# A complex linear attention feeding a mixture of experts on one core: ScalarE's list set by hand through the first attention, first scores in two halves, eight weights by transfers, other steps for the attention of groups four and five

## The chip, the core and the metric

The kernel runs on one core of a Trainium2 chip. Five engines work from queues of their own: TensorE (PE, matrix products; its weight loads are shown apart as PEld), VectorE (DVE), ScalarE (ACT), GpSimd (POOL) and SyncE (SP, which here only issues DMA transfers). The metric is the device time of one execution in microseconds, with the inputs in the chip's memory; three runs of the kernel before took 1015.36 to 1018.92 us, median 1017.08.

## The reference

For each of 4 batches and 8 heads a complex state of 48 x 48 is rotated by a normalised factor at each of 768 steps and takes in one product of a key and a value; the output is the real part read by the query. The outputs of all heads, side by side, are 3072 tokens of 384 features, which go through four dense experts, weighted by normalised probabilities.

```python
scale = np.minimum(mag, 0.999) / (mag + 1e-06)        # mag = sqrt(a_re**2 + a_im**2)
for t in range(S):
    new_re = ar * S_re - ai * S_im
    new_im = ar * S_im + ai * S_re
    S_re, S_im = (new_re + kv, new_im)                # kv = k_t outer v_t
    y[:, :, t] = np.einsum('bhd,bhde->bhe', q[:, :, t], S_re)
...
for e in range(E):
    h = np.maximum(x @ w1[e], 0.0)
    out += p[:, e:e + 1] * (h @ w2[e])
```

## The kernel before

**Products in three parts.** Each fp32 operand of an expert is kept as a rounded high part and a rest (whi and wlo, xha and xla, hh and hl), and each product is three products on TensorE: high with high, rest with high, high with rest. The 16 weight blocks of the first two experts are loaded at the start. Nine of them (NPRE) come by a plain load into wst; split_w casts them on ScalarE (whi, L138), forms the rest on TensorE (lp, the block times the identity minus whi, L147 and L150) and copies it back on ScalarE (wlo, L151). The other seven come by transfers that cast on the way (cast_w), and their rest is formed by a negated copy on ScalarE (L131) on which a second transfer adds the block (add_w).

**Attention in chunks.** The 3072 tokens are 12 groups of 256 tokens, each of two chunks of 128. The front of a group is element-wise. `norm` squares the factors and forms the normalising scale (Ln, Exp and others on ScalarE, the rest on VectorE). `prefix` multiplies the factors along the sequence on VectorE, where pf are its first steps. The head of `finish` forms Q (L425) and the tail K (L441). For groups 2 and later, Q and K go through DRAM (q_d, k_d) by SyncE's transfers and come back with heads on partitions (Qst, Kst); for groups 0 and 1 TensorE turns them instead (qp, and kp with the copy to Kst, L497). Each chunk then has these products on TensorE: ktp (the key turned, L487, copied to KT by ScalarE), dp (the state's increment, L505, subtracted into G), sc (scores, L517, masked by VectorE into scs) and yp (values, L531 and L536, copied to y by ScalarE, L543). For groups 0 to 2, xp (L567) turns y into xha; later groups take y through DRAM into xa. t_factors copies the factors with which `rotate` turns G for the next chunk or group.

**MoE.** moe1 runs experts 0 and 1 over blocks of 256 tokens, one per group, in eight steps: 18 products ph (L179), the rectified copy hh on ScalarE, its rest hl on VectorE, and 12 products po (L198) of a step before. After the 12 blocks of moe1, moe2 runs experts 2 and 3 in blocks of 512 tokens (phb L817, pob L830).

**What sets the order.** The front and the attention of group g run during block g - 1. `between(k)` is called ahead of step k of the block: it advances the front by an estimated cost of STEP per step, and in the steps from FIRST[g] on (2 where the table has no entry) it emits one piece of attention g, of three. Within that, a scheduler with a cost model decides the order in which each engine issues its instructions, except where `behind(a, b)` demands that a is issued after b, on whatever engines they are. Each engine then works through its list strictly in that order, so an instruction that waits holds all behind it. The table WARM names, for some of the last plainly loaded weights, a product of group 0's attention behind which the lp products are put.

The attention of group 0 has nothing beside it, as its output is the first input of the MoE. Between its two chunks stand, on ScalarE, the copies of wlo 6 to 8, the norm of group 1 (tiles s1, u1) and the copies of the attention itself.

Of the kernel before, what the change touches and what calls it, by code (L numbers as in the profile page):

```python
# [15 lines left out]
B, H, S, D = 4, 8, 768, 48  # L16
# [39 lines left out]
NPRE = 9  # L56
WARM = {6: "pq", 7: "tk", 8: "tk1"}
NSEL = 2
XSEL = 3
FIRST = {1: 5, 2: 5, 3: 4, 4: 3}  # L60
# [8 lines left out]
def fast_path(ctx, tc, qkP, aP, vP, probsP, w, out, flag):  # L69
# [159 lines left out]
    with ExitStack() as c1:  # L229
# [81 lines left out]

        def norm(g, A, parts=((0, SEG),), prev=(None, None)):
            s = tmp(f"s{g}")
            u = tmp(f"u{g}")
            for n, (lo, hi) in enumerate(parts):
# [15 lines left out]
                nc.scalar.activation(L, m2, AF.Ln, bias=m2b)  # L331
                exp = nc.scalar.activation(y0, L, AF.Exp, scale=-0.5, bias=lnb)
                if g == 0:
                    nc.vector.tensor_tensor(v, m2, y0, op=ALU.mult)
                    nc.vector.scalar_tensor_tensor(v, v, 4.0 / CAP ** 2, y0, op0=ALU.mult, op1=ALU.mult)
                else:
                    nc.scalar.activation(v, y0, AF.Square, scale=2.0 / CAP)
                    nc.vector.tensor_tensor(v, m2, v, op=ALU.mult)
                nc.scalar.activation(L, y0, AF.Identity, scale=2.0 * EPS / CAP, bias=neg1)
# [50 lines left out]
        def finish(g, A, qk):  # L390
# [24 lines left out]
            def head(lo, hi):  # L415
# [8 lines left out]
                for c in range(2):  # L424
                    ins = nc.vector.tensor_tensor(dst(Q[:, c, :, :C], lo, hi), rows(A[:, c], lo, hi),  # L425
                                                  rows(qk[:, 0], lo, hi), op=ALU.mult)
                    if g < NSEL and lo == 1:
                        behind(ins, red)
                if hi == CG:
                    nc.scalar.activation(Q[:, :, :, C].rearrange("p c (j n) -> p c j n", n=CG),  # L430
                                         A[:, :, SEG - 1, NS - 1::NS].unsqueeze(3).broadcast_to([P, 2, NJ, CG]),
                                         AF.Copy)
# [28 lines left out]
        def t_factors(g):  # L461
            Tr, Ti = Qst[0:D, :, CG - 1, C:], Qst[IM:M, :, CG - 1, C:]
            ins = nc.scalar.activation(TA[0:D], Tr, AF.Copy)
            tc.keep_in_program_order(ins)
            behind(ins, state["y", g])
            tc.keep_in_program_order(nc.scalar.activation(TA[IM:M], Tr, AF.Copy))
            tc.keep_in_program_order(nc.scalar.activation(TB[IM:M], Ti, AF.Copy))
            tc.keep_in_program_order(nc.scalar.activation(TB[0:D], Ti, AF.Copy, scale=-1.0))
# [3 lines left out]
        def chunk(g, c, K, y):  # L472
# [8 lines left out]
            def turned():  # L481
                if last and g >= NSEL:
                    return
                for i in range(2):
                    kt_ps = ps_a.tile([P, HD], F32, tag="pa", name=f"ktp{g}_{c}_{i}")
                    for j in range(NJ):
                        ins = nc.tensor.transpose(kt_ps[:, j * P:(j + 1) * P], K[:, i, j * CG + c, :], ident)  # L487
                    nc.scalar.activation(KT[:, :, i * IM:i * IM + D],
                                         kt_ps.rearrange("p (h d) -> p h d", d=D), AF.Copy)
# [23 lines left out]
            def scores():  # L513
                for hf in range(2):
                    s_ps = ps_a.tile([P, 4, C], F32, tag="pa", name=f"sc{g}_{c}_{hf}")
                    for h in range(4):
                        nc.tensor.matmul(s_ps[:, h, :], Kc[:, hf * 4 + h, :], Qc[:, hf * 4 + h, :],  # L517
                                         start=True, stop=True)
# [4 lines left out]
            def values():  # L523
# [18 lines left out]
                for us in ((slice(0, M),) if g < XSEL else (slice(0, D), slice(IM, M))):  # L542
                    state["y", g] = nc.scalar.activation(y[us, :, cs], y_ps[us], AF.Copy)  # L543
# [27 lines left out]
        def near_attention(g, QK):  # L571
# [12 lines left out]
            sc0()  # L584
# [3 lines left out]
            state["tk1"] = turn1()  # L588
# [69 lines left out]
        for _ in norm(0, A[0], parts=halves):  # L658
            pass
        cuts = (1, NS // CG, NS)  # L660

        todo, last = {}, {}
# [64 lines left out]
        for i in range(NPRE):  # L727
            split_w(i, wst[i] if i in wst else stage1(i, PRE), ((ps_o, "po"), (ps_h, "ph")),
                    prev_pe=state.get(WARM.get(i)), prev_lo=state["kst", 0, 0] if i in WARM else None)
# [7 lines left out]
        behind(nc.vector.reduce_sum(prs, pr, axis=mybir.AxisListType.X), last["dve"])  # L737
# [320 lines left out]
```

## Time and profile before

| | before |
|---|---|
| median of three runs | 1017.08 us (1015.36 to 1018.92) |
| the profiled execution | 1015.63 us |
| its span | 1013.9 us |
| TensorE busy | 982.5 us (97%), 6624 products |
| VectorE busy | 591.2 us (58%) |
| ScalarE busy | 363.4 us (36%) |
| first product of the MoE (ph) starts | 57.20 us |
| last wait of TensorE on another engine or a transfer | 0.93 us, ahead of 268.28 us |

A row of the timeline has the start and the duration in us, the engine, the line, the operation, the tiles out<-in, their shapes, and in brackets the idle time of the engine ahead of it with what ended it. A row of the chain of waits has start, duration and what was done; "issue" is time in which the engine waited for nothing that the profile shows. The windows view gives, for each stretch, its length, the busy time and number of instructions of five engines, the granted clock of TensorE (1.00 is full speed), the share of the DMA engines and what they moved in GB/s. Rows of consecutive equal instructions are drawn together (x16), and a duration then runs from the first start to the last end.

### The profile page before, as it was taken

How to read it: one execution, taken by the hardware profiler on the slowest of the kernel's cores; microseconds unless marked ns; L12 is line 12 of the kernel's file. 1: busy time of each engine (PE TensorE's matmuls, PEld its weight loads, DVE VectorE, ACT ScalarE, POOL GpSimd, SP SyncE). 2: the span in 40 equal slices, each digit the busy share in tenths (PEclk: the TensorE clock that was granted, in tenths of full speed). 3: DMA queues.
4: the chain of work that ended last, by engine and by line, in shares of the span. 5: the costliest groups of instructions: out<-in, count | busy, mean ns of one | idle time of the engine just before them, and what ended most of it. 6: DMA issues, size and time to landing. Idle time of an engine off the chain costs nothing.

```text
span 1013.9 us, 16212 instructions
## 1 busy us (share of the span) xinstructions
PE 982.5 (97%) x6624; PEld 924.4 (91%) x6624; DVE 591.2 (58%) x1219; ACT 363.4 (36%) x653; POOL 34.4 (3%) x64
## 2 busy tenths in 40 slices
PE   4799999999999999999999999999999999999997
PEld 2699999999999999999999999989999999999996
DVE  6798988989797989888842363232232222321221
ACT  7746526436263553636332343121111211211110
POOL 5020000000000000000000000000000000000000
PEclk9899999999999999999999999999999999999999
DMA  9474356474554837457171691021030010100001
GB/s 318 148 147 150 82 154 155 154 184 125 149 164 119 213 99 196 129 145 198 54 164 33 232 334 41 1 88 38 1 125 1 32 63 1 63 1 1 32 1 35
DMA packets 78932, 110.78 MB, mean 109 GB/s; under 512 B 5440, under 2 KB 63344, under 8 KB 78848
## 3 DMA queue, kind: packets, MB, share of 16 engines
q1 hardware_dynamic: 74560, 94.53, 32.6%
q0 software_dynamic: 4288, 15.13, 5.0%
q8 instruction: 54, 0.88, 0.4%
q14 instruction: 30, 0.25, 0.1%
HBM read 73.71 MB, written 35.92 MB: 108 GB/s over the span
## 4 chain that ended last, share of the span: by engine, by line
PE 87%; DVE 4%; DMA 3%; ACT 2%; issue 1%; SPq 0%; DVEq 0%; ACTq 0%
PE pob L830 20%; PE phb L817 20%; PE ph L179 18%; PE po L198 17%; PE sc L517 5%; PE dp L505 2%; PE yp L536 2%; PE yp L531 2%; DMA Kst<-k_d 2%; PE ktp L487 1%; PE xp L567 1%; DMA k_d<-K 1%; DVE K L441 1%; PE qp L385 0%; DVE hl L189 0%
## 5 line engine op out<-in xcount | busy, mean ns | idle before, releaser
L823 DVE SCALAR_TENSOR_TENSOR hlb<-phb,hhb 128x512 fp32r<-128x512 f32 x96 | 66.4, 691 | 270.6 <-ACT hhb L822 270.6
L822 ACT ACTIVATE hhb<-phb 128x512 fp32r<-128x512 f32 x96 | 57.4, 598 | 314.6 <-PE phb L817 299.2
L830 PE MATMUL pob<-wlo,hhb 128*128 128x384 f32 x384 | 129.2, 337 | 0.0
L198 PE MATMUL po<-whi,hh 128*128 128x384 f32 x384 | 129.0, 338 | 0.0
L830 PE MATMUL pob<-whi,hhb 128*128 128x384 f32 x384 | 128.9, 336 | 0.0
L198 PE MATMUL po<-wlo,hh 128*128 128x384 f32 x384 | 128.8, 335 | 0.0
L198 PE MATMUL po<-whi,hl 128*128 128x384 f32 x384 | 124.4, 338 | 0.2 <-DVE hl L189 0.2
L830 PE MATMUL pob<-whi,hlb 128*128 128x384 f32 x384 | 120.4, 336 | 0.0
L188 ACT ACTIVATE hh<-ph 128x512 fp32r<-128x512 f32 x96 | 57.2, 596 | 158.3 <-PE ph L179 158.0
L179 PE MATMUL ph<-xha,whi 128*128 128x256 f32 x576 | 104.9, 287 | 0.8 <-ACT xha L166 0.8
L179 PE MATMUL ph<-xha,wlo 128*128 128x256 f32 x576 | 101.3, 283 | 0.0
L179 PE MATMUL ph<-xla,whi 128*128 128x256 f32 x576 | 101.0, 283 | 0.0
L189 DVE SCALAR_TENSOR_TENSOR hl<-ph,hh 128x512 fp32r<-128x512 f32 x96 | 66.1, 688 | 53.5 <-ACT hh L188 53.0
L817 PE MATMUL phb<-xhb,whi 128*128 128x512 f32 x288 | 91.8, 392 | 0.0
L179 PEld LDWEIGHTS ph<-xha,whi 128*128 128x128 f32 x576 | 86.1, 190 | 1.8 <-ACT xha L166 1.0
L179 PEld LDWEIGHTS ph<-xha,wlo 128*128 128x128 f32 x576 | 82.8, 190 | 0.5 <-issue 0.5
L179 PEld LDWEIGHTS ph<-xla,whi 128*128 128x128 f32 x576 | 82.8, 191 | 0.0
L817 PE MATMUL phb<-xlb,whi 128*128 128x512 f32 x288 | 82.7, 392 | 0.0
L817 PE MATMUL phb<-xhb,wlo 128*128 128x512 f32 x288 | 82.3, 393 | 0.0
L830 PEld LDWEIGHTS pob<-whi,hhb 128*128 128x128 f32 x384 | 72.1, 188 | 3.7
L830 PEld LDWEIGHTS pob<-wlo,hhb 128*128 128x128 f32 x384 | 72.1, 188 | 3.3
L198 PEld LDWEIGHTS po<-whi,hh 128*128 128x128 f32 x384 | 72.5, 189 | 0.5 <-issue 0.3
(165 smaller groups left out, 1574.8 us busy)
## 6 DMA issues: line engine op xcount, KB each, us to landing
wst<-w SPq DMA_DIRECT2D x25, 384.0 KB, 6.4
qk<-qkP SPq DMA_DIRECT2D x24, 384.0 KB, 6.5
acc_d<-acc POOLq DMA_DIRECT2D x24, 384.0 KB, 4.4
prev<-acc_d SPq DMA_DIRECT2D x24, 384.0 KB, 4.9
A<-aP SPq DMA_DIRECT2D x22, 384.0 KB, 7.9
q_d<-Q SPq DMA_DIRECT2D x20, 387.0 KB, 3.6
Qst<-q_d SPq DMA_DIRECT2D x20, 387.0 KB, 5.2
k_d<-K SPq DMA_DIRECT2D x16, 384.0 KB, 3.4
```

Source lines behind the costliest of these rows:

```text
L179: ins = nc.tensor.matmul(ph[:, u, :], wt[:, j * P:(j + 1) * P], xt[:, j, :], start=(n == 0), stop=(n == 3 * NJ - 1))
L188: wts["hh"] = nc.scalar.activation(hh, ph, AF.Relu)
L189: nc.vector.scalar_tensor_tensor(hl, ph, 0.0, hh, op0=ALU.max, op1=ALU.subtract)
L198: nc.tensor.matmul(po[t], ht[:, u, t * P:(t + 1) * P], wt[:, HD:], start=(i % FE == 0 and n == 0), stop=(i % FE == FE - 1 and n == 2))
L505: nc.tensor.matmul(d_ps[:, h, :], KT[:, h, :], vc[:, h * D:(h + 1) * D], start=True, stop=True)
L517: nc.tensor.matmul(s_ps[:, h, :], Kc[:, hf * 4 + h, :], Qc[:, hf * 4 + h, :], start=True, stop=True)
L531: ins = nc.tensor.matmul(yo, st[:, o:o + n], Qc[:, o // D, :], start=True, stop=False)
L536: ins = nc.tensor.matmul(yo, vc[:, o:o + n], sc[h // 4][:, h % 4, :], start=first, stop=True)
L817: nc.tensor.matmul(ph, wt[:, j * P:(j + 1) * P], xt[:, j, :], start=(n == 0), stop=(n == 3 * NJ - 1))
L822: nc.scalar.activation(hh, ph, AF.Relu)
L823: nc.vector.scalar_tensor_tensor(hl, ph, 0.0, hh, op0=ALU.max, op1=ALU.subtract)
L830: ins = nc.tensor.matmul(po[t], ht[:, t * P:(t + 1) * P], wt[:, HD:], start=(i % FE == 0 and n == 0), stop=(i % FE == FE - 1 and n == 2))
```

## The change

Four things are changed. On ScalarE, Ln and Exp of group 1's norm are put behind the copy KT of group 0's second chunk and behind y of its first chunk; the first weights' casts are put behind the norm of group 0; and the copies of wlo 6 and 7 are put behind y of the first chunk. In the norm of group 0 the second half of the factors takes ScalarE's square in place of one of two operations of VectorE. The factors of t_factors are behind the copy y of a named chunk, and the sum of probabilities is put behind Q of group 1's head (`last["qp"]`). In group 0 the scores of the first chunk are issued in two halves of four heads, the second behind the turn of the second key. Eight weight blocks in place of nine are split on the chip, and eight in place of seven come by transfers. FIRST puts the attention of group 4 at step 4 in place of 3, and that of group 5 at step 3 in place of 2.

```diff
@@ -53,11 +53,11 @@
 PRE = ("acc", "xh", "xl")
 MID = ("x", "xh", "xl")
 AHEAD = 6
-NPRE = 9
-WARM = {6: "pq", 7: "tk", 8: "tk1"}
+NPRE = 8
+WARM = {6: "pq", 7: "tk"}
 NSEL = 2
 XSEL = 3
-FIRST = {1: 5, 2: 5, 3: 4, 4: 3}
+FIRST = {1: 5, 2: 5, 3: 4, 4: 4, 5: 3}
 STEP = 3.4
 MORE = (1.9, 1.9, 0.5)
 HALF = (2, 3)
@@ -309,6 +309,8 @@
             nc.vector.tensor_tensor(x[:, 0], v1[:, 0], v2[:, 1], op=ALU.subtract)
             nc.vector.tensor_tensor(x[:, 1], v1[:, 1], v2[:, 0], op=ALU.add)
 
+        last = {}
+
         def norm(g, A, parts=((0, SEG),), prev=(None, None)):
             s = tmp(f"s{g}")
             u = tmp(f"u{g}")
@@ -328,15 +330,18 @@
                     behind(ins[0], exp)
                     behind(sq, exp)
                 yield 1.0
-                nc.scalar.activation(L, m2, AF.Ln, bias=m2b)
+                ln = nc.scalar.activation(L, m2, AF.Ln, bias=m2b)
                 exp = nc.scalar.activation(y0, L, AF.Exp, scale=-0.5, bias=lnb)
-                if g == 0:
+                if g == 1:
+                    behind(ln, state["kt", 0, 1])
+                    behind(exp, state["y", 0, 0])
+                if g == 0 and n == 0:
                     nc.vector.tensor_tensor(v, m2, y0, op=ALU.mult)
                     nc.vector.scalar_tensor_tensor(v, v, 4.0 / CAP ** 2, y0, op0=ALU.mult, op1=ALU.mult)
                 else:
                     nc.scalar.activation(v, y0, AF.Square, scale=2.0 / CAP)
                     nc.vector.tensor_tensor(v, m2, v, op=ALU.mult)
-                nc.scalar.activation(L, y0, AF.Identity, scale=2.0 * EPS / CAP, bias=neg1)
+                last["lin"] = nc.scalar.activation(L, y0, AF.Identity, scale=2.0 * EPS / CAP, bias=neg1)
                 yield 0.95
                 nc.vector.scalar_tensor_tensor(y0, v, 3.0, y0, op0=ALU.subtract, op1=ALU.mult)
                 yield 0.95
@@ -426,6 +431,7 @@
                                                   rows(qk[:, 0], lo, hi), op=ALU.mult)
                     if g < NSEL and lo == 1:
                         behind(ins, red)
+                        last["qp"] = ins
                 if hi == CG:
                     nc.scalar.activation(Q[:, :, :, C].rearrange("p c (j n) -> p c j n", n=CG),
                                          A[:, :, SEG - 1, NS - 1::NS].unsqueeze(3).broadcast_to([P, 2, NJ, CG]),
@@ -462,7 +468,7 @@
             Tr, Ti = Qst[0:D, :, CG - 1, C:], Qst[IM:M, :, CG - 1, C:]
             ins = nc.scalar.activation(TA[0:D], Tr, AF.Copy)
             tc.keep_in_program_order(ins)
-            behind(ins, state["y", g])
+            behind(ins, state["y", g, CG - 1 if g < NSEL else 0])
             tc.keep_in_program_order(nc.scalar.activation(TA[IM:M], Tr, AF.Copy))
             tc.keep_in_program_order(nc.scalar.activation(TB[IM:M], Ti, AF.Copy))
             tc.keep_in_program_order(nc.scalar.activation(TB[0:D], Ti, AF.Copy, scale=-1.0))
@@ -485,8 +491,8 @@
                     kt_ps = ps_a.tile([P, HD], F32, tag="pa", name=f"ktp{g}_{c}_{i}")
                     for j in range(NJ):
                         ins = nc.tensor.transpose(kt_ps[:, j * P:(j + 1) * P], K[:, i, j * CG + c, :], ident)
-                    nc.scalar.activation(KT[:, :, i * IM:i * IM + D],
-                                         kt_ps.rearrange("p (h d) -> p h d", d=D), AF.Copy)
+                    state["kt", g, c] = nc.scalar.activation(KT[:, :, i * IM:i * IM + D],
+                                                             kt_ps.rearrange("p (h d) -> p h d", d=D), AF.Copy)
                 return ins
 
             def turned_back():
@@ -510,12 +516,14 @@
                     nc.vector.tensor_tensor(Gt, state[g, c], d_ps, op=ALU.subtract)
                 state[g, c + 1] = Gt
 
-            def scores():
-                for hf in range(2):
+            def scores(halves=(0, 1), prev=None):
+                for hf in halves:
                     s_ps = ps_a.tile([P, 4, C], F32, tag="pa", name=f"sc{g}_{c}_{hf}")
                     for h in range(4):
-                        nc.tensor.matmul(s_ps[:, h, :], Kc[:, hf * 4 + h, :], Qc[:, hf * 4 + h, :],
-                                         start=True, stop=True)
+                        ins = nc.tensor.matmul(s_ps[:, h, :], Kc[:, hf * 4 + h, :], Qc[:, hf * 4 + h, :],
+                                               start=True, stop=True)
+                        if h == 0 and prev is not None:
+                            behind(ins, prev)
                     s_sb = small.tile([P, 4, C], F32, tag="sc", name=f"scs{g}_{c}_{hf}", bufs=4)
                     nc.vector.tensor_tensor(s_sb, s_ps, maskp.unsqueeze(1).broadcast_to([P, 4, C]), op=ALU.mult)
                     sc.append(s_sb)
@@ -540,7 +548,7 @@
                 if g == 0:
                     state["pe"] = ins
                 for us in ((slice(0, M),) if g < XSEL else (slice(0, D), slice(IM, M))):
-                    state["y", g] = nc.scalar.activation(y[us, :, cs], y_ps[us], AF.Copy)
+                    state["y", g, c] = nc.scalar.activation(y[us, :, cs], y_ps[us], AF.Copy)
 
             return turned, turned_back, increment, scores, values
 
@@ -581,11 +589,15 @@
             state["tk"] = turn0()
             state["bk"] = back0()
             inc0()
-            sc0()
+            sc0((0,))
+            if g > 0:
+                sc0((1,))
             yield
             if g == 0:
                 yield trip(f"q_d{g}", Q, Qst, 1)()
-            state["tk1"] = turn1()
+            tk = turn1()
+            if g == 0:
+                sc0((1,), tk)
             back1()
             val0()
             sc1()
@@ -657,9 +669,10 @@
         A.append(load_a(1))
         for _ in norm(0, A[0], parts=halves):
             pass
+        lin = last["lin"]
         cuts = (1, NS // CG, NS)
 
-        todo, last = {}, {}
+        todo = {}
 
         def front(g, A, qk):
             pre = prefix(g, A, cuts if g < NSEL else (1, NS))
@@ -725,8 +738,8 @@
         for _ in norm(1, A[1], prev=(state["kst", 0, 0], last["dve"])):
             pass
         for i in range(NPRE):
-            split_w(i, wst[i] if i in wst else stage1(i, PRE), ((ps_o, "po"), (ps_h, "ph")),
-                    prev_pe=state.get(WARM.get(i)), prev_lo=state["kst", 0, 0] if i in WARM else None)
+            split_w(i, wst[i] if i in wst else stage1(i, PRE), ((ps_o, "po"), (ps_h, "ph")), prev=lin,
+                    prev_pe=state.get(WARM.get(i)), prev_lo=state["y", 0, 0] if i in WARM else None)
         tick = big.tile([1, 1], F32, name="tick")
         nc.gpsimd.tensor_copy(tick, Qst[0:1, 0, 1, 0:1])
         for i in range(NPRE, NF1):
@@ -734,7 +747,7 @@
         x[0] = split_x(0, x[0])
         for _ in todo.pop(0):
             pass
-        behind(nc.vector.reduce_sum(prs, pr, axis=mybir.AxisListType.X), last["dve"])
+        behind(nc.vector.reduce_sum(prs, pr, axis=mybir.AxisListType.X), last["qp"])
         nc.vector.tensor_scalar(prs, prs, 1e-9, None, op0=ALU.add)
         nc.vector.reciprocal(prs, prs)
         nc.vector.tensor_tensor(pr, pr, prs.unsqueeze(2).broadcast_to([P, NT // P, E]), op=ALU.mult)
```

Lines of the kernel after stand 2 to 8 further down than those of before (L331 is L333, L339 is L344, L343 is L348, L488 is L494, L497 is L503, L517 is L523, L543 is L551).

The first place is ScalarE near the start of the program, before, from the linear term of the first half of group 0's norm on (s0 and u0 are the norm's tiles, whi the weights' high parts, lnb and neg1 constants):

```order
L339 ACTIVATE s0_207<-u0_208,neg1_83 128x384
L138 ACTIVATE whi0_502<-wst0_185 128x768
L331 ACTIVATE s0_207<-s0_207,m2b_89 128x384
L138 ACTIVATE whi1_513<-wst1_187 128x768
L343 ACTIVATE u0_208,st_w_161<-u0_208,neg1_83 128x384
L332 ACTIVATE u0_208<-s0_207,lnb_85 128x384
L138 ACTIVATE whi2_524<-wst2_189 128x768
L138 ACTIVATE whi3_535<-wst3_191 128x768
L339 ACTIVATE s0_207<-u0_208,neg1_83 128x384
```

The same place after:

```order
L344 ACTIVATE s0_207<-u0_208,neg1_83 128x384
L333 ACTIVATE s0_207<-s0_207,m2b_89 128x384
L348 ACTIVATE u0_208,st_w_161<-u0_208,neg1_83 128x384
L334 ACTIVATE u0_208<-s0_207,lnb_85 128x384
L342 ACTIVATE u0_208<-u0_208 128x384
L344 ACTIVATE s0_207<-u0_208,neg1_83 128x384
L138 ACTIVATE whi0_502<-wst0_185 128x768
L138 ACTIVATE whi1_513<-wst1_187 128x768
L138 ACTIVATE whi2_524<-wst2_189 128x768
```

Ln, Exp and the linear term of the norm's second half now stand ahead of the first cast, with a square (L342) of u0 added.

The second place is ScalarE between the two keys of group 0, before, from the copy of G for the first chunk on (s1 and u1 belong to group 1's norm):

```order
L508 ACTIVATE G0_0_364<-dp0_0_355 112x384
L331 ACTIVATE s1_488<-s1_488,m2b_89 128x768
L488 ACTIVATE KT_164<-ktp0_1_0_410 128x8x48
L488 ACTIVATE KT_164<-ktp0_1_1_415 128x8x48
L332 ACTIVATE u1_489<-s1_488,lnb_85 128x768
L151 ACTIVATE wlo8_593<-lp8_0_595 128x384
L151 ACTIVATE wlo8_593<-lp8_1_599 128x384
L337 ACTIVATE u1_489<-u1_489 128x768
L339 ACTIVATE s1_488<-u1_489,neg1_83 128x768
L497 ACTIVATE Kst_163<-kp0_1_0_420 112x4x128
L497 ACTIVATE Kst_163<-kp0_1_4_426 112x4x128
L543 ACTIVATE y0_299<-yp0_0_432 112x4x128
```

The same place after:

```order
L514 ACTIVATE G0_0_364<-dp0_0_355 112x384
L494 ACTIVATE KT_164<-ktp0_1_0_403 128x8x48
L494 ACTIVATE KT_164<-ktp0_1_1_408 128x8x48
L333 ACTIVATE s1_488<-s1_488,m2b_89 128x768
L503 ACTIVATE Kst_163<-kp0_1_0_420 112x4x128
L503 ACTIVATE Kst_163<-kp0_1_4_426 112x4x128
L551 ACTIVATE y0_299<-yp0_0_432 112x4x128
L334 ACTIVATE u1_489<-s1_488,lnb_85 128x768
L151 ACTIVATE wlo6_569<-lp6_0_571 128x384
L151 ACTIVATE wlo6_569<-lp6_1_575 128x384
L151 ACTIVATE wlo7_580<-lp7_0_582 128x384
L151 ACTIVATE wlo7_580<-lp7_1_586 128x384
```

The copies of Kst and y now stand behind KT and Ln alone; Exp, the square, the linear term and the copies of wlo come behind y, those of wlo8 are gone, and those of wlo6 and wlo7, which stood ahead of the first of these rows, are among them.

The third place is TensorE at the scores of group 4 in block 3, before (ph3_3 is the fourth step of that block):

```order
L179 MATMUL ph3_3_2554<-xha3_2300,wlo7_580 128x256 x3
L179 MATMUL ph3_3_2554<-xla3_2301,whi7_579 128x256 x3
L505 MATMUL dp4_0_2529<-v4_0_2515,KT_164 112x48 x8
L517 MATMUL sc4_0_0_2540<-Qst_162,Kst_163 128x128 x4
L517 MATMUL sc4_0_1_2547<-Qst_162,Kst_163 128x128 x4
L198 MATMUL po3_0_0_2398<-whi4_546,hh3_2_2478 128x384
```

The same place after, from the fifth step on:

```order
L179 MATMUL ph3_4_2587<-xla3_2293,whi8_592 128x256 x3
L179 MATMUL ph3_4_2587<-xha3_2292,whi9_594 128x256 x3
L179 MATMUL ph3_4_2587<-xha3_2292,wlo9_668 128x256 x3
L511 MATMUL dp4_0_2562<-v4_0_2548,KT_164 112x48 x8
L523 MATMUL sc4_0_0_2573<-Qst_162,Kst_163 128x128 x4
L523 MATMUL sc4_0_1_2580<-Qst_162,Kst_163 128x128 x4
L179 MATMUL ph3_4_2587<-xla3_2293,whi9_594 128x256 x3
L198 MATMUL po3_0_0_2390<-whi6_568,hh3_3_2513 128x384
```

The increment and the scores of group 4 have moved from behind the fourth step's ph products to within those of the fifth, behind 15 ph and 12 po products more; in the same way those of group 5 stand behind 12 ph products more, and those of group 2 behind 24 ph and 12 po. The scores of group 1 stood ahead of the last 16 po products of block 0 and now stand behind all of them.

## The prediction, made before the result was known

> **What bounds the kernel now.** I read the page first, then TensorE's waits, then the timeline, the windows and the chain around each wait. The page:
>
> ```profile
> span 1013.9 us, 16212 instructions
> PE 982.5 (97%) x6624; PEld 924.4 (91%) x6624; DVE 591.2 (58%) x1219; ACT 363.4 (36%) x653; POOL 34.4 (3%) x64
> ...
> DVE  6798988989797989888842363232232222321221
> ```
>
> TensorE is busy for 982.5 of 1013.9 us, so a change that leaves its products alone can win at most the 31 us in which it is idle, and what it loses at a lowered clock. VectorE is nearly full in the first twenty of 40 slices (to 507 us), the stretch in which attention feeds the MoE. After that it is mostly idle. The waits of TensorE that matter here (us in all, times, longest):
>
> ```profile
> PE qp L385 <- DVE Q L425: 6.3, 1, 6.3
> PE sc L517 <- DMA Kst<-k_d: 3.8, 3, 1.8
> PE xp L567 <- ACT y L543: 1.4, 2, 0.7
> ...
> PE sc L517 <- ACT Kst L497: 1.1, 1, 1.1
> ```
>
> Where these waits stand, from TensorE's timeline (start, duration, in brackets the idle time ahead):
>
> ```profile
> 57.20 0.60 PE L179 MATMUL ph<-xha,whi 128*128 128x256 f32 x3
> ...
> 105.62 1.60 PE L567 MATMUL xp<-y,band 112*128 112x128 f32 x12 [0.70 <-ACT y L543]
> ...
> 136.00 2.05 PE L517 MATMUL sc<-Qst,Kst 112*128 112x128 f32 x16 [1.03 <-DMA Kst<-k_d]
> ...
> 158.55 0.62 PE L179 MATMUL ph<-xha,whi 128*128 128x256 f32 x3 [0.80 <-ACT xha L166]
> ...
> 220.84 3.65 PE L517 MATMUL sc<-Qst,Kst 112*128 112x128 f32 x16 [1.84 <-DMA Kst<-k_d]
> ...
> 268.28 3.47 PE L517 MATMUL sc<-Qst,Kst 112*128 112x128 f32 x16 [0.93 <-DMA Kst<-k_d]
> ```
>
> Two readings follow. First, the MoE cannot start before 57.20, so the front of group 0 is a serial price at the start. Second, groups 1 to 5 each bring a short wait, and the last two bring more than the wait: their 16 score products take 3.65 and 3.47 us, where the chain of waits has 1.85 for the same 16 elsewhere (with it a step of the MoE, 18 ph and 12 po). The windows view (last columns: clock, DMA share, GB/s) shows half clock behind group 4's wait:
>
> ```profile
> 163.13 2.08 PE po L198 x12
> 165.21 2.15 PE ph L179 x18
> ...
> 178.74 1.85 PE sc L517 x16
> ```
>
> ```profile
> 221.00:222.00 1.00, 1.00 (x5) 1.00 (x6) 0.00 (x0) 0.00 (x0) 0.00 (x0) 0.50 1.03 396
> ```
>
> So group 4 costs 1.84 + 1.80 and group 5 costs 0.93 + 1.62. The other waits (0.70, 1.03, 0.80) brought no such stretch.
>
> **Part 1, the first norm on ScalarE.** Its list at the start, and what VectorE got from it:
>
> ```profile
> 9.49 0.84 ACT L138 ACTIVATE whi<-wst 128x768 fp32r<-128x768 f32 x1 [1.73 <-DMA wst<-w]
> 10.24 0.60 ACT L331 ACTIVATE s<-s,m2b 128x384 f32<-128x384 f32 x1
> ...
> 12.07 0.60 ACT L332 ACTIVATE u<-s,lnb 128x384 f32<-128x384 f32 x1
> ...
> 27.18 0.52 ACT L416 ACTIVATE s<-A 128x384 f32<-128x384 f32 x1 [2.40 <-DVE A L309]
> ```
>
> ```profile
> 7.44 0.78 DVE L322 CUSTOM_DVE_ANT_0 s<-s 128x384 f32<-128x384 f32 x1
> ...
> 12.71 0.56 DVE L334 TENSOR_TENSOR u<-s,u 128x384 f32<-128x384 f32 x1 [1.38 <-ACT u L332]
> ...
> 17.42 0.56 DVE L354 TENSOR_TENSOR pf<-A 128x384 f32<-128x384 f32 x1
> ```
>
> The weight cast waits 1.73 us for its transfer with half 2's Ln queued behind it. In the new list Ln, the row sum, Exp, Square and the linear term go first. Ln can then start at about 8.25 (VectorE's 7.44 + 0.78), Exp at about 9.4 instead of 12.07, Square at 10.0. VectorE loses its 1.38 wait and one operation like the 0.56 shown, and the first full-width prefix operation moves from 17.42 to about 15.4: **−2.0** for Q and K of group 0, to which TensorE's 6.3 us wait (qp) goes back. The five casts start at 11.0 instead of 9.49. Their weights are needed at 57 us, and the products that use them stand ahead of qp, in time that is idle. A price is hidden here: the seventh cast (whi6) now stands ahead of copies of wlo on ScalarE, and its transfer is issued late:
>
> ```profile
> 13.66 1.29 SPq L116 DMA_DIRECT2D wst<-w  x2
> ...
> DMA to landing us min/median/max: 7.2/7.2/7.3
> ```
>
> 13.66 + 7.3 = 20.96, so ScalarE stands still for about 2 us there; by my count it ends at 24.8, and the head's squares (27.18 now, 2.40 of idle time ahead) come at 25.1. The cover is 0.3 us.
>
> **Part 2, ScalarE between the keys of group 0.** The chain from the scores of chunk 0 to those of chunk 1:
>
> ```profile
> 40.90 1.52 ACT wlo L151 x4
> ...
> 42.81 0.82 ACT s L331
> 43.63 0.76 ACT KT L488 x2
> 44.39 0.82 ACT u L332
> 45.21 0.76 ACT wlo L151 x2
> 45.97 0.73 ACT u L337
> 46.71 0.82 ACT s L339
> 47.53 0.50 ACT Kst L497
> ...
> 53.60 0.61 ACT y L543
> ```
>
> Between the G copy's queue and Kst stand wlo (1.52), Exp (0.82), wlo again (0.76), Square (0.73) and the linear term (0.82): 4.65 us that now come behind Kst or behind y. Ln (0.82) stays. The second half of the first scores goes behind the second turn, so its product (half of 1.85) no longer stands ahead of the turn. Not all of the 4.65 is won: once ScalarE is free, TensorE's own turn, kp, yp and scores set the pace, and each copy back costs a hand-off. Walking the new order with these durations gives y of chunk 0 at 42.7, its xp at 44.5, y of chunk 1 at 47.75 where 53.60 stands now. From there to the first ph it is 3.60 as now (57.20 − 53.60), 51.35: **−5.85** with the 2.0 of part 1, so 3.85 from this part. Bounds of this part: 1.1 (the wait sc <- ACT Kst alone) to 4.65 + 0.9.
>
> The moved work needs a cover too. wlo6 and wlo7 (1.5 us) now follow y of chunk 0, and the first ph that reads them is three steps of 4.23 on. Square and the linear term of group 1 feed VectorE, which still has the finish of group 0. So VectorE's front of group 1 moves by about 0.9 us only, against TensorE's 5.85. That is the main risk, and is priced below.
>
> **Part 3, eight weights by transfers.** One weight load, one whi cast, four product groups and two wlo copies go (0.76 us of ScalarE, in the list above); one copy of 0.7 us and two Pool transfers come. All lie beside the first block. I cost it at nothing; bounds 0 to 0.8, if its wlo (whi8 is read in step 4) were late.
>
> **Part 4, the later attention.**
>
> *Group 1.* All of its turns and scores now stand behind the last product of block 0. In group 0, where nothing lies between either, such hand-offs cost 1.1 (Kst) and 0.7 (y). I take about 0.8 for Kst, 0.6 for KT and 0.65 for y, 2.05 instead of 0.70: **+1.35**, bounds 0 to +1.5. TensorE's lead is then 4.5.
>
> *Group 2.* 24 ph and 12 po products more (2.9 + 2.1 us) stand ahead of the scores. TensorE arrives at 134.97 − 4.5 + 4.95 = 135.4, and keys that landed at 135.96 need to come only 0.5 earlier: the 1.03 goes. The 0.80 at 158.55 becomes about 1.25, since y and xha follow each other with less between. **−0.58**.
>
> *Group 4.* VectorE and the trip through DRAM come last:
>
> ```profile
> 209.08 1.74 DVE K L441 x2
> 210.85 3.83 DMA k_d<-K
> 214.70 6.00 DMA Kst<-k_d
> ...
> 254.28 0.61 ACT hh L188
> ...
> 255.53 1.83 DVE K L441 x2
> ```
>
> 15 ph and 12 po more (3.87 us) stand ahead of the scores. TensorE, 5.08 ahead, arrives at 219.00 − 5.08 + 3.87 = 217.8. The keys come earlier by at least nothing (the 0.9 of group 1 less one hl more ahead of K, priced like one of the two K operations) and at most by TensorE's 5.08. I take 2.0, nearer to VectorE's own 0.9: 220.70 − 2.0 = 218.7, a wait of 0.9 instead of 1.84: **−0.94**. Whether a wait of 0.9 is followed by half clock is open: 0.93 at 268.28 was, 1.03 at 136.00 was not. I keep the stretch.
>
> *Group 5.* Here K at 255.53 follows directly on an hh that follows TensorE's own product, so keys and TensorE move together. The scores stand 12 ph (1.43 us) further on, more than the wait of 0.93. The wait and its stretch go: 0.93 + 1.62 = **−2.55**.
>
> **The sum:** −5.85 + 1.35 − 0.58 − 0.94 − 2.55 = −8.57. The profiled execution took 1015.63 us (span 1013.9, 1.7 around it), so 1007.06. It was 1.45 below the median of the runs shown, 1017.08. Against that median the forecast is **1008.5**.
>
> [...]
>
> **The rivals** (times against the median).
>
> 1. *The transfers stay last.* VectorE's eight and nine tenths in the slices there speak for it: keys of groups 4 and 5 come no earlier relative to TensorE than now, both waits and stretches stay, or as much comes up at group 6. −5.85 + 1.35 − 0.58 = −5.1: 1012.0. Against it: the scores moved by 3.87 and 1.43 in the order.
> 2. *The front of group 0 doesn't move.* The 0.3 us of cover at whi6 is too little, and the head waits on ScalarE; part 1's 2.0 goes: 1010.5.
> 3. *All of it goes.* Keys of group 4 come 3.1 earlier or more. Then 0.9 and 1.80 more are won: 1005.8; without group 1's 1.35, 1004.5.
> 4. *A shorter wait at group 4 keeps full clock*, as the one of 1.03 did: 1.80 more, 1006.7.
> 5. *Slower.* TensorE leads VectorE by five us, and each of five attentions (groups 1 to 5) meets its keys or y late, with a half-clock stretch behind each. At group 4's present price, 1.84 + 1.80, that is 18.2, where these places cost 8.7 now (0.70 + 1.03 + 0.80 + 3.64 + 2.55): +9.5 − 5.85 = +3.65, 1020.7. It turns slower once the five cost more than 14.6, 2.9 each. Against it: 0.70, 1.03 and 0.80 brought no stretch.
> 6. *The list doesn't decide.* TensorE's start is set by VectorE's chain of Q and K alone, and what ScalarE gives up returns at group 1: within 3 us of now.
>
> **How the numbers follow.** Forecast 0.38, rivals 1 to 6: 0.19, 0.10, 0.12, 0.08, 0.05, 0.08. A measurement of this kernel can tell about 0.3%, 3.05 us. Forecast and rivals 1 to 4 lie below 1014.03: faster 0.87; rival 6 is the same, 0.08; rival 5 slower, 0.05. The range leaves out 5 and 6: from 1002.5 (rival 3 with part 2 at its upper bound) to 1014.0 (rival 1 with rival 2).
>
> **What would show it.** Right: first ph near 51.4; half 2's Ln near 8.3 with no weight cast ahead; about 2 us idle on TensorE around group 1's attention with y and KT as releasers; scores of group 5 at 1.85 us without a wait; a wait under 1 us at group 4. Wrong: Kst of group 0's second chunk still after 46; the head's squares later than 26; scores of groups 2 to 5 waiting longer than now with 0.50 behind them. The forecast fails most simply if VectorE cannot follow, so that a lead of 5 us at the first ph is gone at 300 us.

## The result and the profile after

The changed kernel took 1022.95 us (median of 5 runs, 1022.27 to 1025.19) beside 1018.92 for the kernel before on the same chip: ratio 1.0053, 95% interval 1.003 to 1.0076. It is slower by 4.0 us, where 1008.5 had been forecast. The page of the changed kernel:

```profile
span 1020.5 us, 16202 instructions
PE 985.8 (97%) x6618; PEld 924.3 (91%) x6618; DVE 590.4 (58%) x1218; ACT 363.6 (36%) x652; POOL 35.7 (3%) x66
...
PE 84%; DMA 6%; DVE 4%; ACT 3%; issue 1%; DVEq 0%; ACTq 0%; SPq 0%
```

The share of transfers in the chain of waits has doubled, from 3% to 6%. TensorE's waits in the changed kernel (us in all, times, longest):

```profile
PE sc L523 <- DMA Kst<-k_d: 7.2, 4, 3.0
PE qp L390 <- DVE Q L430: 3.0, 1, 3.0
PE xp L575 <- ACT y L551: 2.1, 3, 0.7
...
PE sc L523 <- issue: 1.0, 1, 1.0
PE sc L523 <- ACT Kst L503: 0.8, 1, 0.8
PE kp L502 <- ACT KT L494: 0.6, 1, 0.6
PE ph L179 <- ACT xha L166: 0.6, 1, 0.6
```

The wait for Q at the start has halved, from 6.3 to 3.0. The wait of scores for their keys has nearly doubled, from 3.8 to 7.2. TensorE's timeline of the changed kernel at the first ph and at the scores of groups 3, 4 and 5:

```profile
51.45 0.60 PE L179 MATMUL ph<-xha,whi 128*128 128x256 f32 x3
...
177.08 2.02 PE L523 MATMUL sc<-Qst,Kst 112*128 112x128 f32 x16 [0.97 <-issue]
...
224.14 3.11 PE L523 MATMUL sc<-Qst,Kst 112*128 112x128 f32 x16 [2.98 <-DMA Kst<-k_d]
...
273.04 3.75 PE L523 MATMUL sc<-Qst,Kst 112*128 112x128 f32 x16 [2.79 <-DMA Kst<-k_d]
```

The MoE starts at 51.45, 5.75 us earlier than at 57.20. Then it is all given back, and in these two executions 6.6 us more (4.0 by the medians). The windows view adds up what TensorE did from the first ph to the end, first in the kernel before, then in the changed one:

```profile
57.20:1013.90 956.70, 944.66 (x6368) 894.54 (x6367) 547.43 (x1101) 323.88 (x574) 19.31 (x31) 0.99 0.36 103
```

```profile
51.45:1020.50 969.05, 949.26 (x6368) 895.86 (x6367) 551.05 (x1113) 324.87 (x575) 20.12 (x32) 0.99 0.37 102
```

For the same 6368 products it took 12.35 us longer: 7.75 more idle (19.79 for 12.04) and 4.60 more busy. Of the busy time about 1.7 is clock, half of a stretch of 3.41 us: at the scores of group 5 the half clock (0.50) now lasts two stretches, 6.83 us from 272.64 to 279.47, where there was one, from 268.66 to 272.07. The changed kernel at both ends of them:

```profile
273.00:274.00 1.00, 0.96 (x4) 1.00 (x5) 0.00 (x0) 0.00 (x0) 0.00 (x0) 0.50 1.02 396
...
278.00:279.00 1.00, 1.00 (x5) 1.00 (x4) 0.91 (x3) 0.06 (x1) 0.00 (x0) 0.50 0.03 8
```

Why the keys come late is seen on VectorE. Its timeline ahead of K of group 4, before, and then ahead of K of groups 4 and 5, changed:

```profile
198.30 1.82 DVE L425 TENSOR_TENSOR Q<-A,qk 128x768 f32<-128x768 f32 x2
200.03 0.95 DVE L168 TENSOR_TENSOR xla<-xa,xha 128x768 fp32r<-128x768 f32 x1
...
208.13 0.95 DVE L338 TENSOR_TENSOR u<-s,u 128x768 f32<-128x768 f32 x1
209.00 1.82 DVE L441 TENSOR_TENSOR K<-A,u 128x768 f32<-128x768 f32 x2
```

```profile
198.81 0.96 DVE L168 TENSOR_TENSOR xla<-xa,xha 128x768 fp32r<-128x768 f32 x1 [2.29 <-ACT xha L166]
202.98 1.82 DVE L430 TENSOR_TENSOR Q<-A,qk 128x768 f32<-128x768 f32 x2
210.88 0.96 DVE L343 TENSOR_TENSOR u<-s,u 128x768 f32<-128x768 f32 x1 [0.81 <-ACT u L342]
211.76 1.82 DVE L447 TENSOR_TENSOR K<-A,u 128x768 f32<-128x768 f32 x2
...
250.38 0.96 DVE L168 TENSOR_TENSOR xla<-xa,xha 128x768 fp32r<-128x768 f32 x1 [2.58 <-ACT xha L166]
261.09 1.82 DVE L447 TENSOR_TENSOR K<-A,u 128x768 f32<-128x768 f32 x2
```

xla of group 3 needs the output y of that group back from DRAM. It stood behind Q of group 4 and found its input ready. Now it stands ahead of Q. VectorE's list at that place, before and changed:

```
L510 TENSOR_TENSOR G3_1_2247<-G3_0_2049,dp3_1_2238 112x384
L425 TENSOR_TENSOR Q4_2187<-A4_1624,qk4_2179 128x8x6x16 x2
L168 TENSOR_TENSOR xla3_2301<-xa3_2226,xha3_2300 128x768
```

```
L516 TENSOR_TENSOR G3_1_2239<-G3_0_2041,dp3_1_2230 112x384
L168 TENSOR_TENSOR xla3_2293<-xa3_2218,xha3_2292 128x768
...
L430 TENSOR_TENSOR Q4_2179<-A4_1616,qk4_2171 128x8x6x16 x2
```

So VectorE waits 2.29 us for the trip of y, seen in the changed kernel's chain of waits:

```profile
190.98 3.59 DMA y_d<-y
...
194.63 3.28 DMA xa<-y_d
...
198.81 0.97 DVE xla L168
```

K of group 4 starts 2.8 us later than before (211.76 for 209.00), K of group 5 5.6 later (261.09 for 255.53). At group 4 the stall has a follow-up. Just ahead of K stands u, an operation of the next group's norm, which needs ScalarE's part of that norm; it found it ready before and now waits 0.81 us for it. At group 5 the order of Q and xla is the old one, and xla waits 2.58 us.

### The profile page after: what moved, and what is told of

The parts are those of the page before. It is cut to its first block, busy times and chain, and to the rows that moved or that the text cites. A ratio compares the mean times of both kernels' runs of the same rounds, so it can differ in the third digit from the quotient of the medians.

```text
span 1020.5 us, 16202 instructions
## 1 busy us (share of the span) xinstructions
PE 985.8 (97%) x6618; PEld 924.3 (91%) x6618; DVE 590.4 (58%) x1218; ACT 363.6 (36%) x652; POOL 35.7 (3%) x66
## 4 chain that ended last, share of the span: by engine, by line
PE 84%; DMA 6%; DVE 4%; ACT 3%; issue 1%; DVEq 0%; ACTq 0%; SPq 0%
PE pob L843 20%; PE phb L830 20%; PE ph L179 16%; PE po L198 16%; PE sc L523 5%; PE yp L544 2%; DMA Kst<-k_d 2%; PE yp L539 2%; PE dp L511 2%; DMA k_d<-K 2%; PE ktp L493 1%; PE xp L575 1%; DMA y_d<-y 1%; DMA xa<-y_d 1%; DVE K L447 1%
## 5 line engine op out<-in xcount | busy, mean ns | idle before, releaser
L198 PE MATMUL po<-whi,hh 128*128 128x384 f32 x384 | 130.2, 341 | 0.7 <-ACT hh L188 0.4
L198 PE MATMUL po<-wlo,hh 128*128 128x384 f32 x384 | 129.4, 337 | 0.0
L198 PE MATMUL po<-whi,hl 128*128 128x384 f32 x384 | 124.6, 340 | 0.5 <-DVE hl L189 0.4
```

What stands on the lines that cost most here:

```text
L198: nc.tensor.matmul(po[t], ht[:, u, t * P:(t + 1) * P], wt[:, HD:], start=(i % FE == 0 and n == 0), stop=(i % FE == FE - 1 and n == 2))
```

## The experiments

Theory A: the loss is VectorE's order, with xla of group 3 ahead of Q of group 4. Theory B: where VectorE waits does not matter, its load as a whole sets the keys. Theory C: the later steps of FIRST delay y, its trip, and with it the next keys. Each ratio is to the kernel before, run beside it (35 runs, medians 1019.24, 1019.03 and 1018.86 in the three sets).

| version | ratio | 95% interval |
|---|---|---|
| e8, the changed kernel again | 1.0046 | 1.0025 to 1.0066 |
| e5, list between the keys, halves and eight transfers alone | 1.0045 | 1.0022 to 1.0067 |
| e7, e3 with attention of groups 3, 5, 6 later still | 1.0026 | 1.0010 to 1.0041 |
| e6, before with xla of group 3 ahead of Q of group 4 | 1.0023 | 1.0003 to 1.0043 |
| e1, changed, FIRST as before | 1.0020 | 1.0003 to 1.0037 |
| e10, before with eight transfers alone | 1.0019 | 0.9997 to 1.0041 |
| e2, before with the new FIRST | 0.9993 | 0.9975 to 1.0011 |
| e3, changed, xla of group 3 behind Q of group 4 | 0.9992 | 0.9975 to 1.0009 |
| e4, before with the new norm of group 0 | 0.9985 | 0.9967 to 1.0003 |
| e9, e3 with FIRST as before | 0.9980 | 0.9962 to 0.9999 |
| e11, e3 with attention of group 3 one step later | 0.9976 | 0.9959 to 0.9992 |
| e12, e4 with the new FIRST | 0.9973 | 0.9953 to 0.9994 |

**Is it FIRST or the start?** e1 makes this edit in the changed kernel, e2 the reverse in the kernel before:

```diff
-FIRST = {1: 5, 2: 5, 3: 4, 4: 4, 5: 3}
+FIRST = {1: 5, 2: 5, 3: 4, 4: 3}
```

> The changed kernel with the table FIRST of before; everything at the start stays as changed. Theory A (the loss is VectorE's list: xla of groups 3 and 4 stands ahead of the next group's Q and holds VectorE 2.3 and 2.6 us for a transfer): the list has the same order at group 3 here, so the stall of about 2.3 us stays, K of group 4 starts at 211 to 212 us, and the time is within 2 us of the changed kernel, 3 to 5 us above before. Theory C (the later steps of FIRST delay y of group 4, its transfer and so K of group 5): K of group 5 comes back by about 4 us, and the time is at or below that of before.

> The kernel before with FIRST of the changed one and nothing else. Theory A: xla of group 3 stays behind Q of group 4, no stall there; scores of group 4 stand 12 po (2.1 us) and of group 5 some 10 products later, so the waits of 1.84 and 0.93 us shrink or go, and the time is 1 to 4 us below before. Theory C: y of group 4 comes later, K of group 5 later than 256 us, and the time is 2 us or more above before.

e1 takes 2.3 us more than before; by the ratios it is 0.26% below the changed kernel (e8), with intervals that overlap. VectorE still waits 1.41 us at xla of group 3, as theory A says. At group 4, other than the expectation says, xla stands behind Q in the changed kernel already (Q at 245.97, xla at 250.38). In e1 it no longer waits there, so the second stall of the changed kernel (2.58) needs the new FIRST. K of group 5 starts at 261.36, but the profiled execution, the slowest of twelve, was late before that: the second K of group 3 starts at 171.96, in the changed kernel at 167.84. From K of group 4 to K of group 5 e1 takes 44.39 us, the changed kernel 49.33 and the kernel before 46.53. So neither theory has its time (A said 3 to 5 us above before, C at or below it). The stall of group 3 stays, for A; beside it the new FIRST probably has a share in the loss, for C. e2 is 0.9 us below before, and its interval holds 1; its waits were 0.95 at scores 4 and 1.91 at scores 5, where K came at 256.08. So in the kernel before the new FIRST does no harm, against C, but moves a wait from group 4 to group 5 rather than removing it.

**Is it the order on VectorE?** e3 takes the stall out of the changed kernel, and e6 puts it into the kernel before.

```diff
                 if k == max(end, nk - 1) and g in x and g >= NSEL:
-                    x[g] = split_x(g, x[g])
+                    while g in (3, 4) and ("Q", g + 1) not in state:
+                        advance(0.5, g + 1)
+                    x[g] = split_x(g, x[g], state.get(("Q", g + 1)) if g in (3, 4) else None)
```

The loop goes on with the next group's front until its Q is issued, and split_x then puts xla behind that Q. For group 4 this is the order that the changed kernel has already.

> The changed kernel, with xla of groups 3 and 4 issued on VectorE behind Q of groups 4 and 5. Theory A: the waits of VectorE for xha (2.3 and 2.6 us) go, K of group 4 starts at 209 to 210 and K of group 5 at 255 to 257 (211.8 and 261.1 in the changed kernel), the wait of scores 5 falls from 2.8 to under 1 us, and the time falls by 4 to 7 us against the changed kernel, to 1 to 3 us below before. Theory B (VectorE's whole load sets the keys; where it waits in its list does not matter): K comes no earlier than 211 and 260, time within 1.5 us of the changed kernel.

VectorE in e3:

```profile
202.79 0.95 DVE L168 TENSOR_TENSOR xla<-xa,xha 128x768 fp32r<-128x768 f32 x1
208.97 1.82 DVE L451 TENSOR_TENSOR K<-A,u 128x768 f32<-128x768 f32 x2
210.70 0.95 DVE L346 TENSOR_TENSOR u<-s,u 128x768 f32<-128x768 f32 x1
...
247.21 0.96 DVE L168 TENSOR_TENSOR xla<-xa,xha 128x768 fp32r<-128x768 f32 x1 [0.91 <-ACT xha L166]
255.48 1.82 DVE L451 TENSOR_TENSOR K<-A,u 128x768 f32<-128x768 f32 x2
```

K of both groups is back where it was before (208.97 and 255.48), scores 4 don't wait, and the median is 1017.51: 1.7 below before, where the changed kernel is 4.0 to 4.3 above. By the ratios (e8 and e3) the edit is worth 5.4 per mille, some 5.5 us. Not all of it is the stall itself: u now stands behind K. From the second K of group 3 to K of group 4 e3 takes 3.9 us less than the changed kernel, of which the stall of 2.29 is the larger part, and u with its wait of 0.81 the rest. One thing came otherwise: scores 5 still wait 3.03. The likely reason is that scores 4 now run early enough for TensorE to be there first. The edit also puts scores 4 behind 3 ph and 7 po more, which may have a share in the gain.

e6 leaves the scores where they were: only the head of group 4 (XL holds the 4) is put behind xla of group 3, which `state` keeps. A few operations of VectorE and ScalarE beside it change places.

```diff
+                    if g in XL and c == 0 and ("xl", g - 1) in state:
+                        behind(red, state["xl", g - 1])
```

> The kernel before with one thing changed on VectorE: the head of group 4 is issued behind xla of group 3, as the changed kernel has it. Theory A: VectorE waits 1.5 to 2.5 us at that xla, K of group 4 starts 1.5 to 2.5 us later than 209.0, the wait of scores 4 grows from 1.84 to 3.3 to 4.3 us, time 1.5 to 4 us above before. Theory B (only VectorE's load counts): K of group 4 within 0.5 us of 209.0, time within 1 us of before.

```profile
201.73 0.96 DVE L169 TENSOR_TENSOR xla<-xa,xha 128x768 fp32r<-128x768 f32 x1 [1.29 <-ACT xha L167]
...
213.59 0.96 DVE L340 TENSOR_TENSOR u<-s,u 128x768 f32<-128x768 f32 x1 [1.67 <-ACT u L339]
214.47 1.82 DVE L445 TENSOR_TENSOR K<-A,u 128x768 f32<-128x768 f32 x2
```

```profile
227.31 3.75 PE L521 MATMUL sc<-Qst,Kst 112*128 112x128 f32 x16 [4.18 <-DMA Kst<-k_d]
```

The wait of scores 4 is 4.18 for 1.84, and the median rises by 3.5 us. In the profiled execution, the slowest but one of twelve, K comes 5.5 later; 2.8 of it arises between the second K of group 3 and K of group 4. The other 2.7 were there already at group 3, behind a half-clock stretch of 3.4 us (0.50 in the whole microseconds from 137 to 139) in that execution. What is new between those two K is mainly VectorE's wait of 1.29 at xla and one of 1.67 at u, the follow-up seen in the changed kernel: the operation s (L324), from which ScalarE works for u, starts at 207.16 for 202.17 before. So the order costs, by the wait at xla and by what it pushes back behind it. Theory B falls with both.

**Which part turns the order?** e4 is the kernel before with the new norm of group 0 alone:

```diff
-                if g == 0:
+                if g == 0 and n == 0:
...
-            split_w(i, wst[i] if i in wst else stage1(i, PRE), ((ps_o, "po"), (ps_h, "ph")),
+            split_w(i, wst[i] if i in wst else stage1(i, PRE), ((ps_o, "po"), (ps_h, "ph")), prev=lin,
```

> The kernel before with only group 0's norm put ahead of the weight casts on ScalarE (half 2 with ScalarE's square); the order of all engines after that is as before. Theory A, and part 1 of the prediction: VectorE and TensorE both move 2.0 us earlier and keep their distance, first ph at 55.2, the waits of groups 1 to 5 as before within 0.5 us, time 1.5 to 2.5 us below before. Theory B: VectorE takes the 2 us back before group 5, waits grow by 1 us or more, time within 1 us of before.

e5 is the changed kernel without these two edits and with FIRST as before:

> The changed kernel with FIRST as before and without the part on group 0's norm (list between the keys of group 0, scores in halves and eight transfers alone). Theory A: TensorE's lead alone puts xla of group 3 ahead of Q of group 4 on VectorE, as in the changed kernel; first ph at 53.3, VectorE waits 1.5 to 2.5 us for xha of group 3, K of group 4 no earlier than 211, time 1 to 5 us above before. Theory C (FIRST is to blame): without the new FIRST it is 2 to 4 us below before.

e10 is the kernel before with the eight transfers alone:

```diff
-NPRE = 9
-WARM = {6: "pq", 7: "tk", 8: "tk1"}
+NPRE = 8
+WARM = {6: "pq", 7: "tk"}
```

> The kernel before with eight weights split and eight by transfers, nothing else. Prediction's part 3: first ph 0 to 0.8 us earlier, time within 1.5 us of before. Rival: the scheduler's order moves with it (scores of group 3 stand 18 ph earlier and those of group 2 some 17 products earlier), so scores 2 or 3 wait 1 to 3 us longer for their keys and the time is 1.5 to 4 us above before.

In e5 xla of group 3 stands ahead of Q and waits 1.67, K of group 4 starts at 213.06, and the loss is there, 3.6 us. In e2, e4 and e10 it stands behind Q. So the list between the keys with the halves makes the order turn, with the eight transfers beside it, which don't alone; the list without them was not run. e4 keeps xla where it was before and is 1.9 us below before, near part 1's 2.0: first ph at 55.14, K of group 4 at 206.91. Its interval still holds 1. The waits were to stay within 0.5 us, and that was wrong: the keys did not land 2 us earlier, as the trip took 4.32 + 6.83 us for 3.83 + 6.00, and scores 4 waited 3.09.

e10 was costed at nothing and came out 1.6 us above before, with 1 inside the interval. Its scores 2 waited 2.17 (1.03 before), a po waited 1.94 for hl, and scores 4 and 5 waited 2.07 and 3.40. K of group 4 starts at 211.90, as late as in the changed kernel, though VectorE waits only 0.16 at xla there. So keys can come late in other ways than by the stall. In e3 and e9 the same eight transfers go with K at 209, so they don't explain the changed kernel's loss by themselves. Whether they cost anything alone stays open; in this program they move the order too.

**What is the lead worth with the stall gone?** e9, e11 and e7 are e3 with other tables. e9 has that of before:

```diff
-FIRST = {1: 5, 2: 5, 3: 4, 4: 4, 5: 3}
+FIRST = {1: 5, 2: 5, 3: 4, 4: 3}
```

> The changed kernel with xla of group 3 behind Q of group 4 and FIRST as before. It tells whether TensorE's lead is worth anything without the later steps. Theory A with a floor (keys of groups 4 and 5 come when VectorE and the trip allow, 209 and 255 us at K, whatever TensorE's lead): scores 4 stand 18 ph and 10 po earlier than in e3, so the wait there is 3 to 5 us with a half-clock stretch, and the time is 1 to 4 us above e3, within 2 us of before. Rival (the lead is a plain gain once the stall is gone): time as e3, 1 to 3 us below before.

e9 took 0.9980. From its timelines:

```profile
51.47 0.60 PE L182 MATMUL ph<-xha,whi 128*128 128x256 f32 x3
...
221.62 3.55 PE L527 MATMUL sc<-Qst,Kst 112*128 112x128 f32 x16 [2.55 <-DMA Kst<-k_d]
```

```profile
208.66 1.82 DVE L451 TENSOR_TENSOR K<-A,u 128x768 f32<-128x768 f32 x2
```

TensorE starts 5.73 us ahead of before, and K of group 4 comes 0.3 ahead. So the floor that was expected is there, though the wait is 2.55, not 3 to 5. At scores 5 (267.86 for 268.28) nearly all of the lead is spent: at group 1's hand-offs, at scores 3 (1.50) and at scores 4. By the ratios e9 can't be told from e3; that it would be 1 to 4 us slower was wrong, and the later steps of FIRST show no use here. e1 is the same program with xla of group 3 ahead of Q. It stands 0.4% above e9, and their intervals don't touch: the order of VectorE once more, with another FIRST (scores 4 stand 10 ph and 3 po earlier in e9).

e11 has group 3 at step 5, e7 also group 5 at step 4 and group 6 at step 3:

```diff
-FIRST = {1: 5, 2: 5, 3: 4, 4: 4, 5: 3}
+FIRST = {1: 5, 2: 5, 3: 5, 4: 4, 5: 3}
```

> The version e3 (xla of group 3 behind Q of group 4, FIRST as changed) with the attention of group 3 one step later (step 5). The wait of 1.2 us at scores 3 goes; y of group 3 is later by about 2 us, which has cover as xla stands behind Q. Theory A: 0.5 to 2 us below e3. Theory C (later attention delays the next block's input): VectorE waits 1.5 us or more for xha of group 3 again, 1 to 3 us above e3.

> The changed kernel with xla of groups 3 and 4 behind Q of the next group, and the attention of groups 3 and 5 one step later still and that of group 6 at step 3 (FIRST 5, 5, 5, 4, 4, 3). Theory A: with the stall gone only the distance between keys and scores is left; the waits at scores 3 (1.2) and 5 (3.0 with a half-clock stretch of 1.7) go and nothing else is late, time 3 to 6 us below e3, 5 to 8 below before. Theory C: later attention delays y and xa, so VectorE waits for xha of groups 4 or 5 by 2 us or more, and the time is not below e3.

e11 is the fastest built on the changed kernel, 1016.41, 2.45 below the kernel before beside it; its interval overlaps that of e3. Scores 3 and 4 no longer wait, scores 5 wait 2.91 and scores 6 1.51. e7 goes one step further and shows the other end of the window:

```profile
300.60 1.01 PE L182 MATMUL ph<-xha,whi 128*128 128x256 f32 x3 [6.28 <-ACT xha L166]
```

```profile
300.58 0.96 DVE L168 TENSOR_TENSOR xla<-xa,xha 128x768 fp32r<-128x768 f32 x1 [3.71 <-ACT xha L166]
```

The waits at scores 4 and 5 are down to 0.74 and 0.63, but y of group 5 is now so late that the whole of TensorE waits for its trip, 6.28 us. Here theory C is right: in e11, with groups 5 and 6 one step earlier, TensorE has no wait between 280 and 305 us, here it has this one.

**Two parts alone.** e12 is the kernel before with the new norm of group 0 and the new FIRST, and nothing of the list between the keys.

> The kernel before with two parts of the change only: the norm of group 0 ahead of the casts, and FIRST. Both leave xla of group 3 behind Q of group 4. Theory A: the two add, 1.9 and 0.7: 2 to 3.5 us below before, first ph at 55.1, wait at scores 4 under 2 us. Rival (the keys' trip through DRAM sets scores 4 and 5, so the 2 us are taken back there): 0 to 1 us below before.

1017.21 us, 0.9973: 1.7 us by the medians, 2.8 by the ratio. The two parts add up within what can be told (0.15% and 0.07% alone). It is faster than before, though its interval ends close to 1, and by the two ratios some 0.7% faster than the changed kernel. In the profiled execution, near its slow end (1019.51), scores 2, 4 and 5 still waited 1.67, 1.63 and 2.10, each with a stretch of half clock (3.4 us at 0.50).

**The changed kernel again** (e8):

> The changed kernel once more, beside the others on one chip: 3 to 5 us above before, 4 to 7 above the version with xla behind Q; the waits at scores 4 and 5 of 2 to 3 us come again, the half-clock stretches behind them in one or two lengths of 3.4 us.

```profile
224.74 2.02 PE L523 MATMUL sc<-Qst,Kst 112*128 112x128 f32 x16 [1.78 <-DMA Kst<-k_d]
```

It was 4.3 us above before again. Scores 4 waited 1.78 here and ran at full clock (1.00), scores 5 waited 2.59 with two stretches of half clock (6.8 us at 0.50); the order and both stalls (1.73 and 2.60) were the same.

## Why the prediction was wrong, step by step

**Parts 1 and 2, the start: right.** First ph 51.45 for 51.35; half 2's Ln at 8.26, Exp at 9.38, y of the second chunk at 47.85 for 47.75. ScalarE stood still 2.17 us for whi6's transfer, and the head's squares began at 25.06 as counted. The work behind y found its cover.

**Group 1: right.** 0.78 for Kst, 0.64 for KT, 0.70 for y: 2.12, forecast 2.05.

**Group 2: missed by 1.** The 1.03 was to go and 0.98 was there; the 0.80 was to become 1.25 and became 0.70 + 0.58. The keys came no earlier: K of group 2 started at 125.15, where it had been 124.62 and 126.42 for the two chunks.

**Group 4: this step failed.** "The keys come earlier ... I take 2.0": K came 2.8 later, and the keys landed at 224.01, where 218.7 was forecast. Its bounds, nothing and 5.08, left out a loss. TensorE's own arrival was off too: 221.16 for 217.8, as 1.7 of its lead of 5.08 was left by then. But keys as late as before (220.70) would have been there in time for that, so the whole wait of 2.98 is the keys' delay. VectorE had gained 0.6 us at the last K of group 1 (85.14 for 85.76) and 0.2 at that of group 3, less than the 0.9 that was counted on. The step took VectorE's list for the one of before with one hl more. It compared TensorE's and ScalarE's lists at the places of the change and not VectorE's ahead of K, where xla had moved past Q. e3 and e9 take this order out and e6 puts it in, and K and the time follow each time. Each of these edits moves some neighbours too, so the size of the stall alone is not shown to better than a few us.

**Group 5: failed with it.** That "keys and TensorE move together" held neither way: K came 5.6 later, by the stall of group 3 and the second one. The second needs the new step of group 4 (e1), probably because y comes later with it. The wait of 0.93 and its stretch were to go (−2.55); the wait came to 2.79, with two stretches that cost about 1.7 each.

**Behind these.** Group 3 had no wait before (the prediction's "groups 1 to 5 each" counts two of group 2), was given none, and had 0.97. Group 6 had 0.41, and three hand-offs at 254 to 259 us, while VectorE was late, 1.1. Of the 4.60 us that TensorE was busy longer 2.9 is not clock. The page has its three po rows 2.0 us longer together (130.2, 129.4, 124.6 for 129.0, 128.8, 124.4), some of it by the clock (at scores 5 a po takes 0.52 us at 0.50, 0.34 at 1.00); why stays open. The sign named last in the prediction came true: the first ph of block 5 starts at 303.60 for 298.88, so the lead was gone by 300 us.

**The rivals.** The fifth, slower at 1020.7, had the right sign and half of the mechanism: TensorE's lead meets late keys, with half clock behind. It took VectorE as standing still where it moved back. With the stall gone (e9) VectorE does stand still, and the 5.7 us at the start are worth 1.5 to 2. That is the mechanism of the first rival, which priced the gain at 5.1. The forecast was of the wrong kind even without the stall: it took a start that helps TensorE for one that helps VectorE too. The one part that moved both, the norm, came out 1.9 us faster by the medians (e4), with 1 in its interval.

## What to carry to other kernels

Here one engine feeds another through a loop (VectorE's keys, a trip through DRAM, scores, y, a trip back). Time won at the start, which did not move the engine that sets the loop, counted only in part: 5.7 us at the first product were worth 1.5 to 2 with the stall gone (e9, where K of group 4 came 0.3 us earlier). In such a loop look for that engine's output, not for the first product. And when a scheduler decides the order, compare the lists of every engine between the change and the next wait, above all where an operation that needs a transfer may have moved ahead of one that doesn't (xla ahead of Q, a wait of 2.29 us). Moving work later had two ends here: the wait of scores 5 for their keys fell from 3.03 us (e3) to 0.63 (e7), and in e7 the next block waited 6.28 us for y.

## What the runs showed of the hardware

From 20 to 340 us, in the profiles that show the clock there (before, changed, e3 to e12, of which e4 from 100 on), half clock began in or just behind waits of TensorE, and the length of the wait alone does not tell when. A stretch lasted 3.41 us (before, 220.87 to 224.28 at 0.50) or twice that (changed, 272.64 to 279.47); in e3 to e12 the windows add up to 3.4 or 6.8 us each. At 0.50 that is about 1.7 us of loss for each 3.4. Waits of up to 0.89 us never had half clock behind them. Of those from 0.92 to 2.10 us some had one stretch (0.93, 1.22, 1.84, 2.10) and some none (0.97, 1.47, 1.78, 2.07). After the first ph all 12 from 2.17 to 6.28 us had one or two. Ahead of it the wait for Q had two in e3 (2.92), one in the changed kernel (3.03) and none in e8 (2.47), e11 (2.71) and e12 (3.07). The changed kernel had a stretch at scores 4 in one execution (2.98 us of wait) and not in another (1.78). Executions of one unchanged kernel lay between 1014.42 and 1025.15 us; the profile that the forecast started from was near the fast end of that.
